# Two split operands of attention: k held twice and rounded whole, with fewer buffers for streamed weights, on one Trainium2 core

## The chip, the cores and the metric

The kernel runs on one core of a Trainium2 chip. The metric is the device time of one execution in microseconds (us); the time shown of a kernel is the median of its runs.

## The reference

Three layers follow one another, all in float32. `moe2_b` and the weights come scaled, which changes no step.

```python
# attention: B, H, S, D = 4, 8, 576, 64; blocks of 64 keys
scores = q @ k.T / sqrt(64)               # per batch and head
scores = where(i // 64 >= j // 64, scores, -1e9)
attn = exp(scores - max); attn = attn / (sum + 1e-9)
x = (attn @ v) -> (2304, 512)
# first layer
h = x @ w_in            # 512 -> 2048
x = maximum(0.01 * h, h) @ w_out          # 2048 -> 512
# second layer
h = x @ w_in
P = a0 + a1*h + a2*h**2 + a3*h**3
Q = 1 + |b0|*|h| + |b1|*h**2
x = (P / (Q + 1e-6)) @ w_out              # (2304, 512)
```

## The kernel before, in words

**Split operands.** The tensor engine multiplies in a rounded form of float32 (F32R). To keep accuracy an operand is split into a high part (rounded) and a low part (what is left, rounded), and a product is made of three matmuls: high by high, high by low, low by high. Weights arrive as int32 pairs; `convert` (L662) loads a block of 512 KB into `cs`, scales its two words, joins them into `cl` on DVE (`cl<-cs`), rounds `cl` to the high part and subtracts for the low part. For the first layer the high parts stay on chip (`w1i`, `w1o`) and the low parts go out to DRAM (`W1L`). For half of the second layer's weights both parts go to DRAM (`W2H`, `W2L`): the high part through a tile `ch`, of which there are two.

**Attention.** There are 32 heads. Heads 0 to 7 (`n < NSF`) are multiplied in plain float32 from tiles `fq` and `fk`. Heads 8 to 31 are split: `load_qk` (L717) loads q into partitions 0 to 63 and k into partitions 64 to 127 of one of two tiles `qk`, and `a1` (L752) makes four tiles from them. QT has the scaled q, rounded, in its lower half of the partitions and its low part in the upper. KH has the rounded k in both halves, made by two operations of 64x576. QM and KL have the rounded q and the low part of k in their lower halves. These tiles take over the storage of `fq` and `fk`, so the trace calls them `split_fq` and `split_fk`. Then `a2_part` makes the scores in tiles `T`, their negated maxima `nm` and the exponentials `PB`; `a2_norm` divides `PB` by its sums `sm`; `a3a` and `a3b` transpose `PB` on PE and evacuate the result (into `acc` for the plain heads, into `pTh` and `pTl` for the split ones); `a4` multiplies with v, which is held in `vr`, or `VHL` when split; `xh` and `xl` are the two parts of the attention's output.

**First layer.** `moe1` (L924) is called for 160 units of twelve matmuls each into a tile `M`: a unit is 128 columns of `w_in` or of `w_out`, for one batch of 512 rows. The last 64 rows of each batch, 256 together, are done at the end, in units of 256 columns (the left-over stage). Every unit streams its low weights, 256 KB, from `W1L` into a tile `wl`; there are six of them. The results `gh` and `gl` of the first half feed the second, whose sums are kept in `acc`, and `x2hd` and `x2ld` in DRAM take the layer's output in two parts.

**Second layer.** `moe2` (L1007) is an ordinary loop. Its first rows come back as `x2h` and `x2l` (1 MB each) while the first layer still runs.

**What sets the order.** Attention, the conversions and the first layer aren't issued as they are written. A recorder keeps every operation with a key (`rec.key`) and, where more than one engine can do it, its forms (`rec.either`). Before they are scheduled, `amend(AMEND)` (L346) steps through a table of entries `step:key:lax:form`: so many operations further on, a number is added to the key or to the leeway, or one form, and so an engine, is fixed. `schedule` then puts the operations in order with a model of costs, and `issue` (L493) writes them out; every recorded instruction therefore bears line L503 in the trace, and its tiles tell it apart. All DMAs of this part go through SP's queue in the order that the schedule gave.

Of the kernel before, what the change touches and what calls it, by code (L numbers as in the profile page):

```python
# [12 lines left out]
F32 = mybir.dt.float32  # L13
F32R = mybir.dt.float32r
# [20 lines left out]
}  # L35

AMEND = """
# [21 lines left out]
"""  # L59


# [465 lines left out]
def attention_moe_moe_kernel(  # L527
# [14 lines left out]
    nc = rec  # L542
    P = 128
    B, H, D, S = q.shape
# [3 lines left out]
    KD = DM // P  # L548
# [19 lines left out]
    def pool(stack, group="all", **kw):  # L568
        return rec.pool(stack, group, **kw)
# [12 lines left out]
    ap = pool(att, "att", name="ap", bufs=1, side="right")  # L582
    xp = pool(ctx, name="xp", bufs=2)
    w1 = pool(ph1, name="w1", bufs=1)
    mp = pool(ph1, name="mp", bufs=2)
    cp = pool(ph1, name="cp", bufs=2)
# [5 lines left out]
    coef = const.tile([P, 6], F32, name="coef")  # L592
    cq = const.tile([P, 1], F32, name="cq")[:, 0:1]

    qk = [ap.tile([P, S], F32, name=f"qk{e}") for e in range(2)]
    vr = [ap.tile([P, 5, P], F32, name=f"vr{j}") for j in range(2)]
    xs = vr[1].rearrange("p t d -> p (t d)")[:, 0:S]

# [5 lines left out]
    QT, QM, KH, KL = {}, {}, {}, {}  # L604
# [31 lines left out]
    NSF = 8  # L636
    E1 = "pvpap"
# [20 lines left out]
    def load_block(i):  # L658
        stage[i] = cp.tile([P, 512, 2], I32, tag="cs", name="cs", bufs=3)
        nc.sync.dma_start(out=stage[i].rearrange("p (r n) w -> p r (n w)", r=KD), in_=blocks[i][0])  # L660

    def convert(i, load, key):  # L662
        rec.key = load
        load_block(i)
        rec.key, rec.lax = key, LAX[0]
        s = stage.pop(i)
        hi, lo = s[:, :, 1], s[:, :, 0]
        nc.scalar.activation(
            hi.bitcast(F32), hi.bitcast(F32), AF.Prelu, scale=2.0 ** -112, alpha=-(2.0 ** 32)
        )  # L670
        rec.either(
            ("ACT", "activation", (lo, lo.bitcast(U32), AF.Copy), {"scale": 0.875 * 2.0 ** -29, "bias": 0.4375}),
            ("POOL", "tensor_scalar", (lo, lo.bitcast(U32), 0.875 * 2.0 ** -29, 0.4375, ALU.mult, ALU.add), {}),
        )
        rec.lax = LAX[1]
        _, (dh, dl), kept = blocks[i]
        f = cp.tile([P, KD, P], F32, tag="cl", name="cl", bufs=3)
        fl = f
        if isinstance(dh, int):
            wh, fl = (  # L680
                x[:, 512 * dl:512 * (dl + 1)].rearrange("p (r c) -> p r c", c=P) for x in W2[dh]
            )
            kept = 2
        else:
            wh = dh if kept else cp.tile([P, KD, P], F32R, tag="ch", name="ch", bufs=2)
        hi, lo = (x.rearrange("p (r c) -> p r c", c=P) for x in (hi, lo))
        nc.vector.scalar_tensor_tensor(
            f.bitcast(I32), hi, 3, lo, ALU.logical_shift_left, ALU.bitwise_or
        )
        rounded(wh, f, "av")  # L690
        subtract(fl if kept == 2 else f.bitcast(F32R), f, wh.bitcast(F32))
        for d, t in () if kept == 2 else ((dh, wh.bitcast(F32)), (dl, f))[kept:]:
            nc.sync.dma_start(out=d, in_=t, also=((), (rec.token("w", i),)))
        rec.lax = 0.0
# [22 lines left out]
    def load_qk(n, second=None):  # L717
        if n >= NHD:
            return
        b, h = divmod(n, H)  # L720
        if n < NSF:
            dq, dk = (T[0:D, :] for T in plain[n % 4])
        else:
            dq, dk = qk[n % 2][0:D, :], qk[n % 2][D:P, :]
        rec.key = LOADKEY(n)
        for c in (slice(0, 192), slice(192, S)) if n == 0 else (slice(0, S),):
            nc.sync.dma_start(out=dq[:, c], in_=q[b, h][:, c])
            (second or nc.sync).dma_start(out=dk[:, c], in_=k[b, h][:, c])

    def load_v(p):  # L730
        b, j = divmod(p, NP)
# [6 lines left out]
    def subtract(out, a, b):  # L738
        rec.either(*((e, "tensor_tensor", (out, a, b, ALU.subtract), {}) for e in ("DVE", "POOL")))

    def rounded(out, in_, engines, by=1.0):
        forms = {
            "a": ("ACT", "activation", (out, in_, AF.Copy), {"scale": by}),
            "v": ("DVE", "tensor_scalar", (out, in_, by, None, ALU.mult), {}),
            "p": ("POOL", "tensor_scalar", (out, in_, by, 1.0, ALU.mult, ALU.mult), {}),
        }
        rec.either(*(forms[e] for e in engines))

    def cp1(eng, out, in_, by=1.0):
        return rounded(out, in_, CH, by)  # L750

    def a1(n):  # L752
        if n < NSF:
            if n > 0:
                fq = plain[n % 4][0][0:D, :]
                cp1("a", fq, fq, SCALE)
            return
        if n < NSF + 2:
            split_tiles(n)
        e = n % 2  # L760
        qs, ks = qk[e][0:D, :], qk[e][D:P, :]
        cp1(E1[0], QT[e][0:D, :], qs, SCALE)
        nc.vector.scalar_tensor_tensor(
            QT[e][D:P, :], qs, SCALE, QT[e][0:D, :].bitcast(F32), ALU.mult, ALU.subtract
        )
        cp1(E1[2], QM[e][0:D, :], QT[e][0:D, :].bitcast(F32))
        cp1(E1[3], KH[e][D:P, :], ks)
        cp1(E1[4], KH[e][0:D, :], ks)
        subtract(KL[e][0:D, :], ks, KH[e][D:P, :].bitcast(F32))

    def a1v(n):
        e = n % 2
# [151 lines left out]
    def moe1(u, load, key):  # L924
        g, kind, i, d = units[u]
        xh, xl = X[g]
        n = NT1 if g < B else B * NL
        if kind == "in":
            wh, s = w1i[:, :, i * P:(i + 1) * P], i
        else:  # L930
            wh, s = w1o[:, 4 * i:4 * i + 4, d * P:(d + 1) * P], NF + 4 * i + d
        rec.key = load
        wl = mp.tile([P, 4, P], F32R, tag="wl", name="wl", bufs=6)
        nc.sync.dma_start(out=wl.bitcast(F32), in_=W1L[s], also=((rec.token("w", BLOCK[s]),), ()))
        rec.key, rec.line = key, 1
        T = psS.tile([P, 512], F32, tag="S", name="M")[:, 0:n]
# [194 lines left out]
    def LOADKEY(n):  # L1131
        return n - 2.8 if n > 2 else n - 20.0
# [3 lines left out]
    for n in range(3):  # L1136
        load_qk(n, nc.scalar)
# [104 lines left out]
    for i in range(len(blocks)):  # L1242
        convert(i, block_key(i) - 1.5, block_key(i))
# [22 lines left out]
    nc = tc.nc  # L1266
# [48 lines left out]
```

## Time and profile before

| | before |
|---|---|
| median of 3 runs | 991.14 us (990.75 to 991.68) |
| the profiled execution | 990.94 us |
| its span | 989.2 us |
| mean granted clock of TensorE | 1.00 |
| PE busy | 977.1 us (99%) |
| DVE, ACT, POOL busy | 735.3, 672.2, 317.6 us |
| DMA traffic | 140.95 MB, 142 GB/s over the span |

The span goes from the first to the last instruction of the profiled execution; what is beyond it in the execution's time is start and end. A trace lists for every instruction when it ran, on which engine, from which tiles, and what ended the idle time before it. PE is the matmul engine, PEld its weight load, DVE, ACT and POOL the three others that compute, SP the one that issues DMAs (SPq is its queue). L503 is the line of the recorder. A group's row gives the instructions' count, their summed busy time and the mean of one in ns.

### The profile page before, as it was taken

The numbers are of one execution on the slowest core, as the hardware profiler recorded it, in microseconds if no ns is written. First come the engines' busy times: TensorE is split into PE (matmuls) and PEld (weight loads), VectorE is DVE, ScalarE is ACT, GpSimd is POOL, SyncE is SP. The second block draws the span as 40 slices with busy tenths as digits, with TensorE's granted clock in tenths as the row PEclk, the third lists the DMA queues.
The fourth block names the chain that finished last, engine by engine and source line by source line (L and its number), as shares of the span: only waits on it lengthen the run. The fifth ranks groups of instructions, "written<-read, shape, count | busy, mean of one in ns | idle before, by whom it ended". The sixth has DMA issues, their size and how long they took to land.

```text
span 989.2 us, 14611 instructions
## 1 busy us (share of the span) xinstructions
PE 977.1 (99%) x4980; PEld 827.1 (84%) x4980; DVE 735.3 (74%) x1244; ACT 672.2 (68%) x1381; POOL 317.6 (32%) x352
## 2 busy tenths in 40 slices
PE   9989999999999999999999999999999999999998
PEld 6768888888888888888888998888888888888896
DVE  5889988887776677555523118999888888888886
ACT  7998989877877667445422328776766766676775
POOL 6778688676654555115203330000000000000000
PEclk9999999999999999999999999999999999999999
DMA  9967878797774542249734759120102101010010
GB/s 207 286 201 240 273 237 272 246 336 229 246 237 143 164 115 69 66 116 328 229 97 125 234 144 386 58 86 0 43 1 86 43 1 43 1 43 1 1 43 23
DMA packets 94923, 140.95 MB, mean 142 GB/s; under 512 B 10368, under 2 KB 47488, under 8 KB 94848
## 3 DMA queue, kind: packets, MB, share of 16 engines
q1 hardware_dynamic: 94368, 139.32, 45.1%
q8 instruction: 39, 0.64, 0.3%
q10 hardware_dynamic: 480, 0.70, 0.2%
q14 instruction: 36, 0.29, 0.1%
HBM read 108.53 MB, written 31.46 MB: 142 GB/s over the span
## 4 chain that ended last, share of the span: by engine, by line
PE 93%; ACT 3%; DMA 2%; DVE 1%; issue 1%; POOL 0%; SPq 0%; ACTq 0%; POOLq 0%; DVEq 0%
PE M L503 40%; PE h L1028 20%; PE o L1082 20%; PE T L503 13%; ACT PB L503 2%; DMA fq<-in_q_dram 1%; DMA vr<-in_v_dram 0%; ACT cs L503 0%; ACT acc L503 0%; POOL PB L503 0%; SPq L503 0%; DMA qk<-in_q_dram 0%; DVE nm L503 0%; DVE xl L503 0%; DVE pTl L503 0%
## 5 line engine op out<-in xcount | busy, mean ns | idle before, releaser
L503 PE MATMUL M<-gh,w1o 128*128 128x512 f32 (+1 forms) x320 | 120.0, 376 | 0.1
L503 PE MATMUL M<-gh,wl 128*128 128x512 f32 (+1 forms) x320 | 118.1, 369 | 0.0
L503 PE MATMUL M<-gl,w1o 128*128 128x512 f32 (+1 forms) x320 | 118.0, 370 | 0.0
L1040 ACT ACTIVATE ea<-h,coef 128x512 f32<-128x512 f32 (+1 forms) x80 | 51.6, 645 | 88.0 <-PE h L1028 88.0
L503 ACT ACTIVATE gf<-M 128x512 f32<-128x512 f32 (+1 forms) x80 | 44.2, 555 | 85.6 <-PE M L503 77.6
L503 ACT ACTIVATE PB<-T,nm 128x448 f32<-128x448 f32 (+4 forms) x160 | 82.6, 524 | 27.6 <-DVE nm L503 27.1
L503 DVE TENSOR_TENSOR acc<-M,acc 128x512 f32<-128x512 f32 (+1 forms) x60 | 38.1, 635 | 71.1 <-PE M L503 70.8
L1028 PE MATMUL h<-x2l,w2h 128*128 128x512 f32 (+1 forms) x240 | 88.3, 368 | 0.0
L1028 PE MATMUL h<-x2h,w2l 128*128 128x512 f32 (+1 forms) x240 | 88.3, 368 | 0.0
L1028 PE MATMUL h<-x2h,w2h 128*128 128x512 f32 (+1 forms) x240 | 88.2, 368 | 0.0
L503 DVE TENSOR_REDUCE nm<-T 128x1 f32<-128x192 f32 (+4 forms) x160 | 71.4, 482 | 19.9 <-PE T L503 19.2
L503 POOL TENSOR_TENSOR gl<-gf,gh 128x512 fp32r<-128x512 f32 (+1 forms) x44 | 50.0, 1137 | 107.5 <-ACT gh L503 97.1
L1082 PE MATMUL o<-w2h,g2h 128*128 128x512 f32 x216 | 84.2, 390 | 0.0
L1082 PE MATMUL o<-w2l,g2h 128*128 128x512 f32 x216 | 84.2, 390 | 0.0
L1082 PE MATMUL o<-w2h,g2l 128*128 128x512 f32 x216 | 84.0, 389 | 0.0
L1043 DVE SCALAR_TENSOR_TENSOR ea<-eh,coef,ea 128x512 f32<-128x512 f32 (+1 forms) x80 | 55.6, 695 | 31.3 <-ACT eh L1041 30.3
L503 PE MATMUL M<-xh,w1i 128*128 128x512 f32 x256 | 75.4, 399 | 0.0
L503 PE MATMUL M<-xl,w1i 128*128 128x512 f32 x256 | 73.3, 391 | 0.0
L503 PE MATMUL M<-xh,wl 128*128 128x512 f32 x256 | 73.1, 391 | 0.0
L503 PEld LDWEIGHTS M<-gl,w1o 128*128 128x128 f32 x320 | 60.3, 189 | 10.5
L503 PEld LDWEIGHTS M<-gh,w1o 128*128 128x128 f32 x320 | 60.4, 189 | 9.0 <-ACT gh L503 0.4
L503 PEld LDWEIGHTS M<-gh,wl 128*128 128x128 f32 x320 | 60.4, 189 | 8.7
(147 smaller groups left out, 2581.1 us busy)
## 6 DMA issues: line engine op xcount, KB each, us to landing
wl<-w1l SPq DMA_DIRECT2D x160, 256.0 KB, 2.9
cs<-in_moe_w_in_dram SPq DMA_DIRECT2D x32, 512.0 KB, 5.4
cs<-in_moe_w_out_dram SPq DMA_DIRECT2D x32, 512.0 KB, 5.2
w1l<-cl SPq DMA_DIRECT2D x32, 256.0 KB, 4.2
vr<-in_v_dram SPq DMA_DIRECT2D x16, 256.0 KB, 3.9
w2h<-ch SPq DMA_DIRECT2D x16, 256.0 KB, 5.3
w2l<-cl SPq DMA_DIRECT2D x16, 256.0 KB, 3.7
x2hd<-xo SPq DMA_DIRECT2D x16, 256.0 KB, 2.9
```

Source lines behind the costliest of these rows:

```text
L503: getattr(self.eng[o.engine], o.name)(*a, **k)
L1028: nc.tensor.matmul(h[:, 0:n], lhsT=a, rhs=x, start=(kk == 0 and i == 0), stop=(kk == KD - 1 and i == 2))
L1040: nc.scalar.activation(a, h, AF.Abs, scale=coef[:, 4:5])
L1043: nc.vector.scalar_tensor_tensor(a, h2, coef[:, 5:6], a, ALU.mult, ALU.add)
L1082: nc.tensor.matmul(ob[t], lhsT=a, rhs=w, start=(f == 0 and i == 0), stop=(f == NF - 1 and i == 2))
```

## The change

In place of one tile with q below and k above, there are a tile `qx` for q and a tile `kk` that k is loaded into twice, once in each half of the partitions. The high part of k is rounded by one operation of 128x576, and the low part is taken from the lower halves. `ch` has one buffer in place of two, `wl` four in place of six. The table AMEND is written anew; its rows are cut here.

```diff
--- before.py
+++ after.py
@@ -35,27 +35,79 @@
 }
 
 AMEND = """
-0:40 3:-17 6:-37 1:11 16:878 3:-154 21:-538 2:-349 7:-126 3::86 3::194 4::62 1::48 4::41 6::78:0 1::79:0 1:::1
...
-1:-252 1:-252 1:-252 1:-252 1:-252 1:-252 1:-252 1:-252 1:-252 1:-252 1:-252 18::81 1::38 15::77 343::10 2::46
+0:40 1:98 1:8 1:14 13:276 1:276 1:276 1:276 18:-23 2:-23 1:-32 3:-59 1:-23 1:-25:567 1:326 1:1 1:43:16 1:-112 1:-592:3
...
+1:-242 1:-242 1:-242 1:-242 1:-242 1:-242 1:-242 1:-75 1:-142
 """
 
 
@@ -592,7 +644,8 @@
     coef = const.tile([P, 6], F32, name="coef")
     cq = const.tile([P, 1], F32, name="cq")[:, 0:1]
 
-    qk = [ap.tile([P, S], F32, name=f"qk{e}") for e in range(2)]
+    qx = [ap.tile([P, S], F32, name=f"qx{e}") for e in range(2)]
+    kk = [ap.tile([P, S], F32, name=f"kk{e}") for e in range(2)]
     vr = [ap.tile([P, 5, P], F32, name=f"vr{j}") for j in range(2)]
     xs = vr[1].rearrange("p t d -> p (t d)")[:, 0:S]
 
@@ -682,7 +735,7 @@
             )
             kept = 2
         else:
-            wh = dh if kept else cp.tile([P, KD, P], F32R, tag="ch", name="ch", bufs=2)
+            wh = dh if kept else cp.tile([P, KD, P], F32R, tag="ch", name="ch", bufs=1)
         hi, lo = (x.rearrange("p (r c) -> p r c", c=P) for x in (hi, lo))
         nc.vector.scalar_tensor_tensor(
             f.bitcast(I32), hi, 3, lo, ALU.logical_shift_left, ALU.bitwise_or
@@ -721,11 +774,13 @@
         if n < NSF:
             dq, dk = (T[0:D, :] for T in plain[n % 4])
         else:
-            dq, dk = qk[n % 2][0:D, :], qk[n % 2][D:P, :]
+            dq, dk = qx[n % 2][0:D, :], kk[n % 2][0:D, :]
         rec.key = LOADKEY(n)
         for c in (slice(0, 192), slice(192, S)) if n == 0 else (slice(0, S),):
             nc.sync.dma_start(out=dq[:, c], in_=q[b, h][:, c])
             (second or nc.sync).dma_start(out=dk[:, c], in_=k[b, h][:, c])
+        if n >= NSF:
+            nc.sync.dma_start(out=kk[n % 2][D:P, :], in_=k[b, h])
 
     def load_v(p):
         b, j = divmod(p, NP)
@@ -758,15 +813,14 @@
         if n < NSF + 2:
             split_tiles(n)
         e = n % 2
-        qs, ks = qk[e][0:D, :], qk[e][D:P, :]
+        qs = qx[e][0:D, :]
         cp1(E1[0], QT[e][0:D, :], qs, SCALE)
         nc.vector.scalar_tensor_tensor(
             QT[e][D:P, :], qs, SCALE, QT[e][0:D, :].bitcast(F32), ALU.mult, ALU.subtract
         )
         cp1(E1[2], QM[e][0:D, :], QT[e][0:D, :].bitcast(F32))
-        cp1(E1[3], KH[e][D:P, :], ks)
-        cp1(E1[4], KH[e][0:D, :], ks)
-        subtract(KL[e][0:D, :], ks, KH[e][D:P, :].bitcast(F32))
+        cp1(E1[3], KH[e], kk[e])
+        subtract(KL[e][0:D, :], kk[e][0:D, :], KH[e][0:D, :].bitcast(F32))
 
     def a1v(n):
         e = n % 2
@@ -930,7 +984,7 @@
         else:
             wh, s = w1o[:, 4 * i:4 * i + 4, d * P:(d + 1) * P], NF + 4 * i + d
         rec.key = load
-        wl = mp.tile([P, 4, P], F32R, tag="wl", name="wl", bufs=6)
+        wl = mp.tile([P, 4, P], F32R, tag="wl", name="wl", bufs=4)
         nc.sync.dma_start(out=wl.bitcast(F32), in_=W1L[s], also=((rec.token("w", BLOCK[s]),), ()))
         rec.key, rec.line = key, 1
         T = psS.tile([P, 512], F32, tag="S", name="M")[:, 0:n]
```

The order of the instructions moves nearly everywhere. Matmuls stay the same in number (4886), and so do POOL's instructions (357); ACT has 1201 in place of 1229, DVE 1250 in place of 1246, SP 524 in place of 500. The engines of the split heads' k rounding are 13 on ACT, 10 on POOL and 1 on DVE in place of 26, 21 and 2. Three places follow, with rows of the order as the program has them. A row is line, operation, output, inputs and the output's shape; the numbers in names tell tiles apart.

The first is ACT's order around the evacuation of a plain head's first transposes, 128x896 into acc, at about 54 us. Before:

```order
L503 ACTIVATE split_fk2_656<-qk1_96 64x576
L503 ACTIVATE PB04_113,sm_664<-T_644,nm_658 128x576
L503 ACTIVATE PB03_112,sm_664<-T_598,nm_658 128x448
L503 ACTIVATE PB02_111,sm_664<-T_632,nm_658 128x320
L503 ACTIVATE PB00_109,sm_664<-T_639,nm_658 128x64
L503 ACTIVATE PB01_110,sm_664<-T_639,nm_658 128x192
L503 ACTIVATE acc_123<-T_673 128x448
L503 ACTIVATE cs_584<-cs_584 128x512
L503 ACTIVATE w1o_122<-cl_681 128x4x128
L503 ACTIVATE PB04_113<-PB04_113,sm_664 128x576
L503 CAST xh_339<-T_650 64x512
L503 ACTIVATE acc_123<-T_677 128x896
```

Now:

```order
L555 ACTIVATE PB14_120<-PB14_120,sm_564 128x576
L555 ACTIVATE PB04_115,sm_666<-T_648,nm_659 128x576
L555 ACTIVATE PB03_114,sm_666<-T_607,nm_659 128x448
L555 ACTIVATE PB00_111,sm_666<-T_634,nm_659 128x64
L555 ACTIVATE PB02_113,sm_666<-T_626,nm_659 128x320
L555 ACTIVATE PB01_112,sm_666<-T_634,nm_659 128x192
L555 ACTIVATE acc_125<-T_672 128x448
L555 CAST xh_341<-T_654 64x512
L555 ACTIVATE acc_125<-T_683 128x896
```

Ahead of the evacuation (the last row of both) a split_fk rounding, a cs conversion, a w1o rounding and the normalisation of PB04 aren't there any more; the normalisation at the beginning, of PB14, is that of another head and stood two rows above the first one shown.

The second is SP's queue where the first rows of the second layer come back (x2h, x2l), behind 436 us; wl are the low weights of consecutive units, cs weights to convert, and xleft the left-over rows. Before:

```order
L503 DMA cab_92<-in_moe2_a_dram 128x4
L503 DMA xleft1_5019<-xld_63 128x1024
L503 DMA cab_92<-in_moe2_b_dram 128x2
L503 DMA wl_5040<-w1l_64 128x512
L503 DMA x2h_5045<-x2hd_61 128x4x512
L503 DMA x2l_5052<-x2ld_62 128x4x512
L503 DMA wl_5060<-w1l_64 128x512
L503 DMA wl_5087<-w1l_64 128x512
L503 DMA cs_5095<-in_moe2_w_in_dram 128x4x256
L503 DMA cs_5101<-in_moe2_w_out_dram 128x1024
L503 DMA wl_5117<-w1l_64 128x512
```

Now:

```order
L555 DMA xleft1_5034<-xld_63 128x1024
L555 DMA cab_92<-in_moe2_a_dram 128x4
L555 DMA cab_92<-in_moe2_b_dram 128x2
L555 DMA wl_5058<-w1l_64 128x512
L555 DMA x2h_5064<-x2hd_61 128x4x512
L555 DMA x2l_5069<-x2ld_62 128x4x512
L555 DMA wl_5079<-w1l_64 128x512
L555 DMA wl_5103<-w1l_64 128x512
L555 DMA cs_5114<-in_moe2_w_in_dram 128x4x256
L555 DMA cs_5120<-in_moe2_w_out_dram 128x1024
L555 DMA wl_5133<-w1l_64 128x512
```

The wl ahead of x2h was that of unit 94 (wl_5040); now it is that of unit 93 (wl_5058), and the one of unit 94 (wl_5079) stands behind x2l.

The third is ACT's order at the last two roundings into ch, at about 279 us. Before:

```order
L503 ACTIVATE PB04_113,sm_3319<-T_3300,nm_3312 128x576
L503 ACTIVATE PB03_112,sm_3319<-T_3332,nm_3312 128x448
L503 ACTIVATE PB02_111,sm_3319<-T_3336,nm_3312 128x320
L503 ACTIVATE pTh_119<-T_3340 128x896
L503 ACTIVATE ch_3370<-cl_3353 128x512
L503 ACTIVATE ch_3377<-cl_3358 128x512
L503 ACTIVATE gf_3385<-M_3351 128x512
L503 ACTIVATE gh_3397<-gf_3385 128x512
```

Now:

```order
L555 ACTIVATE ch_3622<-cl_3526 128x512
L555 ACTIVATE PB12_118<-PB12_118,sm_3427 128x320
L555 ACTIVATE cs_3522<-cs_3522 128x512
L555 ACTIVATE cs_3536<-cs_3536 128x512 x2
L555 ACTIVATE PB04_115,sm_3660<-T_3633,nm_3644 128x576
L555 ACTIVATE PB03_114,sm_3660<-T_3642,nm_3644 128x448
L555 ACTIVATE PB02_113,sm_3660<-T_3648,nm_3644 128x320
L555 ACTIVATE ch_3689<-cl_3668 128x512
```

The two roundings into ch stood next to each other; now seven instructions lie between them (one row holds two).

## Rows read from the trace of the kernel before

**Rows 1.** The page's first line.

```profile
span 989.2 us, 14611 instructions
```

**Rows 2.** Windows: busy us of PE, PEld, DVE, ACT, POOL; clock, DMA share, GB/s.

```profile
50.00:75.00 25.00, 21.43 (x122) 16.40 (x120) 21.61 (x43) 24.32 (x62) 19.14 (x22) 1.00 0.66 203
...
225.00:250.00 25.00, 25.00 (x138) 21.59 (x137) 18.41 (x34) 18.02 (x41) 14.92 (x17) 1.00 0.81 245
...
550.00:575.00 25.00, 25.00 (x211) 25.00 (x210) 3.40 (x8) 8.02 (x20) 6.71 (x11) 1.00 0.69 209
```

**Rows 3.** Timeline of PE: start, us, what, [idle before <- releaser]; 50 to 80 us.

```profile
54.72 1.24 PE L503 MATMUL T<-fk,fq 128*128 128x288 f32 x4 [1.54 <-ACT acc L503]
...
63.00 0.66 PE L503 MATMUL T<-ident,PB 128*128 128x128 f32 x4 [0.97 <-ACT PB L503]
...
68.53 2.09 PE L503 MATMUL T<-ident,PB 128*128 128x128 f32 x14 [0.43 <-DVE acc L503]
...
71.06 3.08 PE L503 MATMUL T<-acc,vr 128*128 128x128 f32 x12 [0.44 <-ACT acc L503]
...
78.79 1.06 PE L503 MATMUL T<-ident,PB 128*128 128x128 f32 x8 [1.16 <-DVE acc L503]
```

**Rows 4.** Groups by form of ACT, 0 to 110 us: busy, mean ns | idle.

```profile
L503 ACT ACTIVATE cs<-cs 128x512 f32<-128x512 f32 x21 | 14.3, 686 | 0.1
...
L503 ACT ACTIVATE acc<-T 128x896 f32<-128x896 f32 x7 | 6.5, 927 | 0.4 <-PE T L503 0.3
...
L503 ACT ACTIVATE PB<-PB,sm 128x576 f32<-128x576 f32 x7 | 5.5, 789 | 0.0
L503 ACT ACTIVATE w1i<-cl 128x512 fp32r<-128x512 f32 x8 | 5.1, 642 | 0.0
...
L503 ACT ACTIVATE acc<-T 128x320 f32<-128x320 f32 x6 | 2.6, 434 | 0.0
...
L503 ACT ACTIVATE fq<-fq 64x576 f32<-64x576 f32 x3 | 2.0, 678 | 1.3 <-DMA fq<-in_q_dram 1.3
L503 ACT ACTIVATE PB<-PB,sm 128x448 f32<-128x448 f32 x3 | 2.0, 674 | 0.3 <-DVE sm L503 0.3
...
L503 ACT ACTIVATE PB<-PB,sm 128x64 f32<-128x64 f32 x5 | 1.8, 358 | 0.0
...
L503 ACT ACTIVATE split_fk<-qk 64x576 fp32r<-64x576 f32 x2 | 1.4, 680 | 0.1
```

**Rows 5.** Groups by form of DVE, 0 to 110 us.

```profile
L503 DVE SCALAR_TENSOR_TENSOR cl<-cs 128x512 int32<-128x512 int32 x20 | 18.1, 915 | 0.5 <-DMA w1l<-cl 0.2
```

**Rows 6.** Groups by form over the span: the roundings of k.

```profile
L503 POOL TENSOR_SCALAR split_fk<-qk 64x576 fp32r<-64x576 f32 x21 | 18.0, 857 | 5.8 <-DVE pTl L503 4.1 <-POOL cl L503 0.2
L503 ACT ACTIVATE split_fk<-qk 64x576 fp32r<-64x576 f32 x25 | 17.1, 683 | 5.2 <-PE T L503 4.6
```

**Rows 7.** PE's waits: us in total, times, longest.

```profile
PE T L503 <- POOL PB L503: 1.3, 2, 0.9
```

**Rows 8.** Timeline of PE in unit 94.

```profile
452.48 0.39 PE L503 MATMUL M<-gh,w1o 128*128 128x512 f32 x1
452.71 0.39 PE L503 MATMUL M<-gh,wl 128*128 128x512 f32 x1
```

**Rows 9.** The loads of wl issued from 549 to 583 us: duration ns, landing us.

```profile
L503 SPq DMA_DIRECT2D wl<-w1l x24: 319/319/319, 549.5 to 582.5; - x24
...
DMA to landing us min/median/max: 2.5/2.7/3.8
```

**Rows 10.** Timeline of SP behind 439 us.

```profile
439.27 0.37 SPq L503 DMA_DIRECT2D x2h<-x2hd  x1
...
441.79 3.05 SPq L503 DMA_DIRECT2D wl<-w1l  x2
```

**Rows 11.** DMA issues from 441.7 to 442.1 us: KB, us to landing.

```profile
wl<-w1l SPq DMA_DIRECT2D x1, 256.0 KB, 8.9
```

**Rows 12.** DMA issues from 200 to 300 us: KB, median us to landing.

```profile
w2h<-ch SPq DMA_DIRECT2D x13, 256.0 KB, 5.2
```

90 rows, old and new, of the table AMEND are left out of this document.

## The prediction

> **What bounds the kernel now.** I read the page's first line and the busy shares by stretch first, then the timeline of PE, then the list of what PE waited for, and last the busy groups of ACT, DVE and POOL. The profiled execution took 990.94 us, of which 989.2 are the span [rows 1]; the median of the runs is 991.14, so 0.2 us are added to every sum below to reach a median. From about 125 us on PE is busy all the time: 25.00 of 25 us in the attention stretch and in the left-over stage [rows 2], and the change leaves its matmuls as they are. So nothing after that is to be gained, unless PE begins it earlier. In the stretch from 50 to 75 us it is another engine that ends last: ACT is busy 24.32 of 25 us and PE 21.43 [rows 2]. The timeline of PE shows where that comes through: five waits, 1.54, 0.97, 0.43, 0.44 and 1.16 us, 4.54 together, three of them for ACT's evacuations (acc) or normalisations (PB), two for DVE's evacuations [rows 3]. Each us that ACT and DVE have less to do ahead of these five places starts all the later matmuls earlier.
>
> **The change part by part.**
>
> *One rounding of k instead of two.* Of each split head (24 of them) two 64x576 roundings go, 0.683 us where ACT does one and 0.857 where POOL does [rows 6], and one of 128x576 comes. No row has that; the nearest is ACT's normalisation of the same shape, 0.789 [rows 4]. Its bounds are 0.683, if only the columns count, and 1.54, the two old ones together. I take 0.79, so a head saves 0.75 us and 24 heads 18 us of engine time. Nearly all of it lies behind 125 us, where PE waits for no one [rows 2], and is worth nothing there. What counts is the part ahead of the five waits, and what the new order does with the rest.
>
> *Work ahead of the five waits.* I counted ACT's and DVE's instructions up to the one that releases PE, in the order before and in the new one, and priced the differences.
> - Release of the wait at 54.72 (the 128x896 evacuation): 83 instructions ahead before, 79 now. Two cs conversions fewer (-1.37), one fq (-0.68), one split_fk and one split_fq (-0.68 each), one PB 128x576 (-0.79), one w1i rounding (-0.64); one PB 128x64 (+0.36), one acc 128x320 (+0.43), one acc 128x896 (+0.93) more [rows 4]. Sum -3.1 us.
> - Release at 63.00 (PB 128x192): two cs (-1.37), one fq and four split roundings of 64x576 (five of 0.68, -3.4) fewer; one PB 128x576, one 128x448, one 128x64 (+0.79, +0.67, +0.36) and one acc 128x896 (+0.93) more; a w1i less and a w1o more cancel [rows 4]. Sum -2.0 us.
> - Release at 71.06 (128x896): counted in the same way, with three w1i roundings fewer in place of one, -3.7 us.
> - Release at 78.79 (DVE): eight instructions fewer ahead; two conversions cl<-cs make 1.8 us of it [rows 5], and 0.37 us each for the other six would be enough for what follows.
>
> Each wait is a bound: release plus all the PE work behind it. Today the last one binds, and the bound of an earlier one lies below it by the waits that follow. So the bounds fall by 3.1+3.00 = 6.1 (54.72), 2.0+2.03 = 4.0 (63.00), 3.7+1.16 = 4.9 (71.06) and over 4.0 (78.79); by what stands ahead of 54.72 at most all five waits can go, 4.54. The least counts: **-4.0 us**. The wait at 68.53 I could not price, since PE's own order differs there; its bounds are 0 and 0.43 of this.
>
> *k loaded twice.* 24 more DMAs of 144 KB on SP's queue. At the rate of 50 to 75 us (203 GB/s at a share of 0.66, so 308 at full share) [rows 2] each takes 0.48 us of the DMA engines, 11.5 us in all. PE waits for no DMA anywhere in its list, whose largest entries are engines, with POOL's PB at 1.3 [rows 7]. I cost it at 0; the cover is the second tile, loaded while the other head is at work. If it were gone, one late load would cost PE its 0.48.
>
> *wl from 6 buffers to 4.* A low weight block is now asked for three units ahead instead of five. Of 512-column units three are 36 matmuls, 0.23 apart [rows 8], 8.2 us of cover; in the left-over stage, with 211 matmuls in 25 us [rows 2], a unit is 1.42 us and three are 4.27, against landings of at most 3.8 plus 0.32 to issue [rows 9]. So 0, with 0.15 us to spare: this is the thinnest cover of the change.
>
> *x2 burst behind 439 us.* Today x2h goes out at 439.27, after the load for unit 94; the next wl behind the 2 MB follows at 441.79 [rows 10] and lands 8.9 us later, at 450.7 [rows 11]. In the new order the pair goes out one unit later and the load of unit 94 stands behind it. One unit is 12 x 0.23 = 2.7 us, so it lands at about 453.4 against its first use at 452.71 [rows 8]. Bounds are 0 (the DMA engines are freer by then) and 4.0 (all of the following loads one after another late); I take the shift, rounded down because the queue starts emptier: **+0.5**.
>
> *One ch buffer.* A rounding into ch now waits until the w2h transfer has read the last one, 5.2 us from issue to landing [rows 12]. The order spreads these roundings: the closest pairs have 6, 7 and 8 instructions between them, at about 0.65 us [rows 4] 3.9, 4.6 and 5.2 us. That leaves 1.3+0.6+0 = 2 us of ACT's time, perhaps 4 with the issue. ACT is busy 18.02 of 25 us there [rows 2], so most of it falls into idle time. Between 0 and 4 I take **+0.5**.
> The Trainium skill says under "Trainium Kernel Development and Optimization", section Best Practices, to double-buffer so that DMA overlaps with compute, which speaks against this edit; by that rule the full 4 us would show, rival C. The trace of before has two buffers and cannot show it.
>
> Sum: -4.0+0.5+0.5 = -3.0, from 990.94 to 987.9, as a median 988.1. With the ends of the terms, -4.54 and -2.0, this case alone runs from 986.6 to 989.1.
>
> **The rivals.**
> - **B, the new order keeps it all.** All five waits go, the two later terms are nothing, and the 1.3 us for POOL's PB [rows 7] go too, since POOL also has less k to round: 990.94-4.54-1.3+0.2 = 985.3. For it: POOL's 0.857 is the dearer form [rows 6]. Against: those two waits come ahead of the first split head.
> - **C, the gain is given back behind the attention.** One ch buffer costs its 4 us, or the x2 burst its 4: 990.94-4.0+4.0+0.2 = 991.1; with half of that 989. For it: ACT's and DVE's streams run in order, so a stalled rounding holds the evacuation behind it. Against: PE has not waited there once.
> - **E, the waits only change their place.** The change doesn't do what it seems to: if PE's waits come from the round trip scores, exponential, transposes, evacuation and not from ACT's load, fewer instructions ahead release nothing earlier, and 991 stays. For it: two of the five waits are for DVE, which is less full than ACT. Against: 24.32 of 25 [rows 2].
> - **D, the left-over stage starves (slower).** Four buffers give one unit in (1.42+0.32+L)/4 us, with L from issue to landing. At 3.8 that is 1.39, under 1.42; it decides from L of 3.94 on. At L = 5, which the extra pressure of late loads could bring, a unit takes 1.69, 0.27 more, and over 26 units 7 us: 995. For it: the margin of 0.15 us [rows 9]. Against: the median landing there is 2.7. To come out slower than before it must eat 3 us, so L over 4.4 throughout.
>
> **How the numbers follow.** The forecast has 0.45, B 0.16, C and E 0.13 each, D 0.13. A measurement tells about 0.2%, 2 us, from no change: faster is below 989.2, slower above 993.1. Forecast and B are faster (0.61); of C and E together 0.01 more; the rest of them, 0.25, and 0.01 of D are the same (0.26); D's other 0.12 is slower. So 0.62, 0.26 and 0.12. The range goes from 984.5, a little under B, to 992.0, a little over C and E; it leaves out D and a few hundredths beyond B. The likeliest case's own range is the 986.6 to 989.1 above.
>
> **What would show it.** Right: in the stretch from 50 to 75 us PE's busy time rises above 21.43 toward 24, the waits in [rows 3] shrink to about half a us in all, and the first matmul of a given unit in the second half comes 3 to 4 us earlier; the 128x576 rounding takes about 0.8 us. PE stays at 25.00 of 25 in the left-over stage, and at most about 0.5 us of PE idle stands near unit 94, with ACT or DVE waiting a little for w2h's transfer. Wrong: PE waits on wl in the left-over stage (D); an idle of several us near 450 or waits for ch on ACT that PE's list answers to (C); five waits of the same sum between 50 and 80 us (E); or a rounding of 1.2 us or more, which would take most of the 18 us back.

## The result, and the profile after

The changed kernel takes 996.34 us (median of 6 runs, 995.32 to 998.76), the kernel before 991.24 in the same comparison: a ratio of 1.0055, with a 95% interval of 1.0045 to 1.0065. It is slower by 5 us, where 3 us less were forecast. The profiled execution took 996.11 us, its span is 994.3.

The second layer has no part in it. These are PE's first matmuls of that layer, in the timeline of the kernel before and in that of the changed one:

```profile
591.12 0.40 PE L1028 MATMUL h<-x2h,w2h 128*128 128x512 f32 x1
```

```profile
596.27 0.40 PE L1082 MATMUL h<-x2h,w2h 128*128 128x512 f32 x1
```

They lie 5.15 us apart, and from there to the end both take 398.0. So all of it is lost before. The waits of PE in the changed kernel (what it waited for: us in total, times, longest):

```profile
PE T L555 <- POOL PB L555: 2.8, 2, 2.0
PE T L555 <- ACT PB L555: 2.6, 4, 1.0
PE T L555 <- ACT acc L555: 1.7, 2, 1.3
PE warm L555 <- DVE cq L555: 1.2, 1, 1.2
PE M L555 <- DMA wl<-w1l: 1.1, 1, 1.1
```

And its busy time by stretch, in the columns of [rows 2]; behind it one more stretch of the kernel before:

```profile
50.00:75.00 25.00, 23.03 (x129) 17.72 (x127) 18.12 (x40) 22.62 (x58) 17.09 (x21) 1.00 0.62 186
100.00:125.00 25.00, 23.78 (x127) 19.29 (x126) 22.73 (x39) 19.36 (x44) 15.25 (x15) 1.00 0.77 240
175.00:200.00 25.00, 22.97 (x115) 19.77 (x114) 18.75 (x29) 18.39 (x40) 18.48 (x17) 0.93 0.78 249
225.00:250.00 25.00, 25.00 (x135) 21.60 (x135) 19.63 (x37) 18.70 (x44) 16.57 (x18) 1.00 0.84 268
550.00:575.00 25.00, 25.00 (x204) 24.73 (x203) 3.44 (x8) 7.82 (x19) 8.43 (x10) 1.00 0.77 233
```

```profile
175.00:200.00 25.00, 25.00 (x137) 21.42 (x136) 22.01 (x35) 21.26 (x49) 17.52 (x17) 1.00 0.78 240
```

Against [rows 2] the stretch from 50 to 75 us has gained as meant: PE 23.03 for 21.43, ACT 22.62 for 24.32. What is new is 175 to 200 us, with 2.03 us of PE idle and a granted clock of 0.93, where PE had been busy throughout. The timeline of PE has the places:

```profile
29.68 1.24 PE L555 MATMUL T<-fk,fq 128*128 128x288 f32 x4 [1.30 <-ACT acc L555]
...
62.09 0.66 PE L555 MATMUL T<-ident,PB 128*128 128x128 f32 x4 [0.77 <-ACT PB L555]
63.38 3.08 PE L555 MATMUL T<-acc,vr 128*128 128x128 f32 x12 [0.64 <-ACT PB L555]
...
69.69 3.08 PE L555 MATMUL T<-acc,vr 128*128 128x128 f32 x12 [0.35 <-ACT acc L555]
...
109.81 0.33 PE L555 MATMUL T<-ident,PB 128*128 128x128 f32 x1 [0.96 <-ACT PB L555]
...
184.98 1.93 PE L555 MATMUL T<-ident,PB 128*128 128x128 f32 x8 [2.03 <-POOL PB L555]
...
457.69 0.50 PE L555 MATMUL M<-gh,wl 128*128 128x512 f32 x1 [1.07 <-DMA wl<-w1l]
```

To add up what each place costs, every matmul of a trace is charged with the median spacing of its shape and kind (plain, transposing or split) in the kernel before (0.227 us for one of 512 columns), and PE's lag at a matmul is its start less what the matmuls ahead were charged. The lag in us, by the work that PE has behind it:

| us of PE work done | 20 | 45 | 70 | 100 | 165 | 170 | 430 | 435 |
|---|---|---|---|---|---|---|---|---|
| before | 5.3 | 6.2 | 13.2 | 14.4 | 15.5 | 15.6 | 20.5 | 20.5 |
| changed | 4.3 | 6.9 | 10.7 | 14.3 | 15.7 | 19.6 | 24.3 | 25.6 |
| run dve_order | 4.3 | 7.2 | 11.0 | 12.4 | 14.0 | 14.1 | 21.1 | 22.3 |
| run x2_late | 5.1 | 6.2 | 9.9 | 13.5 | 15.0 | 19.0 | 24.1 | 24.0 |
| run all_three | 4.7 | 6.0 | 9.8 | 11.3 | 12.8 | 12.9 | 18.0 | 18.0 |

Between 45 and 70 the changed kernel loses 3.8 where the one before lost 7.0: the gain is there, 3.2 us. By 100 it is given back (the waits at 28 and 109 us among others). Then 3.9 go at one place, at 183 us, and 1.3 at 457, behind the x2 burst. All the rest runs alike.

What happens at 183 us stands in the timelines of DVE and POOL in the changed kernel:

```profile
173.77 2.40 DVE L555 SCALAR_TENSOR_TENSOR cl<-cs 128x512 int32<-128x512 int32 x1
176.09 0.68 DVE L555 TENSOR_TENSOR acc<-M,acc 128x512 f32<-128x512 f32 x1
176.80 3.39 DVE L555 SCALAR_TENSOR_TENSOR split_fq<-qx,split_fq 64x576 fp32r<-64x576 f32 x1
180.22 0.75 DVE L555 TENSOR_TENSOR vr<-T,vr 64x576 f32<-64x576 f32 x1
...
182.63 0.17 DVE L555 RECIPROCAL sm<-sm 128x5 f32<-128x5 f32 x1
...
183.22 1.27 DVE L555 SCALAR_TENSOR_TENSOR cl<-cs 128x512 int32<-128x512 int32 x2
```

```profile
174.31 1.30 POOL L555 TENSOR_TENSOR cl<-cl,w1o 128x512 fp32r<-128x512 f32 x1
175.57 1.89 POOL L555 TENSOR_TENSOR split_fk<-kk,split_fk 64x576 fp32r<-64x576 f32 x1
177.43 1.29 POOL L555 TENSOR_TENSOR cl<-cl,w1o 128x512 fp32r<-128x512 f32 x1
178.69 0.88 POOL L555 TENSOR_TENSOR VHL<-vr,VHL 128x320 fp32r<-128x320 f32 x1
182.90 2.02 POOL L555 TENSOR_SCALAR PB<-PB,sm 128x448 f32<-128x448 f32 x1 [3.33 <-DVE sm L555]
```

DVE's subtraction for split_fq reads two operands of SBUF. It takes 0.74 us at its quickest in this trace, and 3.39 here. POOL runs three subtractions without a pause, to 179.57, and DVE's ends 0.62 us after that, at 180.19. Everything behind it on DVE is 2.6 us late, sm among it; for sm waits POOL's PB (3.33), and for that PE (2.03). A second hold, of POOL by DVE, adds to it: this normalisation of PB takes 2.02 us, where twelve of its fourteen in this trace take 0.64, and DVE's two conversions at 183.22 lie within it. With 0.64 PE's wait would have been about 0.65 us (an estimate, 2.03 less the 1.38).

The clock makes it dearer. By windows of 2 us (in the columns of [rows 2]):

```profile
182.00:184.00 2.00, 0.95 (x5) 0.45 (x3) 2.00 (x7) 1.73 (x5) 1.10 (x1) 1.00 0.79 251
184.00:186.00 2.00, 1.02 (x5) 1.03 (x6) 0.52 (x2) 2.00 (x7) 1.44 (x2) 0.77 0.75 200
186.00:188.00 2.00, 2.00 (x11) 1.82 (x10) 0.41 (x1) 1.52 (x3) 1.28 (x1) 0.50 0.97 335
188.00:190.00 2.00, 2.00 (x13) 1.82 (x12) 1.74 (x3) 1.83 (x4) 1.12 (x2) 0.88 0.96 338
```

After the idle time PE goes on at the lower of its two levels (1.2 GHz, 0.50) until about 188 us. So 2.03 us of waiting cost 3.9 us of lag. Not every execution pays that: in the profiles of x2l_later and fq_later the same wait (2.00 and 1.99 us) passes at 1.00 and costs 2.3 and 2.4 us. The other runs of the changed kernel agree: those with a mean clock of 0.999 and 1.000 took 995.32 and 995.40, those with 0.997 took 998.25 and 998.76.

### The profile page after: what moved, and what is told of

Read it like the earlier page. It is cut to its first block, busy times and chain, and to the rows that moved or that the text cites. A ratio compares the mean times of both kernels' runs of the same rounds, so it can differ in the third digit from the quotient of the medians.

```text
span 994.3 us, 14617 instructions
## 1 busy us (share of the span) xinstructions
PE 979.2 (98%) x4980; PEld 827.0 (83%) x4980; DVE 740.7 (74%) x1248; ACT 655.0 (66%) x1353; POOL 315.1 (32%) x352
## 4 chain that ended last, share of the span: by engine, by line
PE 88%; DVE 3%; DMA 3%; ACT 3%; issue 1%; SPq 1%; POOL 0%; ACTq 0%; DVEq 0%; POOLq 0%
PE M L555 37%; PE h L1082 20%; PE o L1136 20%; PE T L555 12%; ACT PB L555 2%; DMA fq<-in_q_dram 1%; DMA wl<-w1l 1%; DVE split_fq L555 1%; DVE cl L555 1%; SPq L555 1%; DMA fk<-in_k_dram 0%; DVE nm L555 0%; ACT cs L555 0%; ACT acc L555 0%; DMA qx<-in_q_dram 0%
## 5 line engine op out<-in xcount | busy, mean ns | idle before, releaser
L555 ACT ACTIVATE PB<-T,nm 128x320 f32<-128x320 f32 (+4 forms) x160 | 82.7, 524 | 31.2 <-DVE nm L555 30.7
L555 DVE TENSOR_REDUCE nm<-T 128x1 f32<-128x320 f32 (+4 forms) x160 | 71.2, 482 | 24.3 <-PE T L555 23.6
L555 POOL TENSOR_TENSOR gl<-gf,gh 128x512 fp32r<-128x512 f32 (+1 forms) x46 | 54.7, 1192 | 75.3 <-ACT gh L555 54.4
L555 PE MATMUL T<-ident,PB 128*128 128x128 f32 x480 | 65.0, 278 | 5.0 <-POOL PB L555 2.8
```

The lines of the kernel that those rows point to most:

```text
L555: getattr(self.eng[o.engine], o.name)(*a, **k)
```

## The experiments

Two theories. **Theory 1:** the new order costs, by DVE held behind POOL, with the x2 burst as a loss of its own. **Theory 2:** the parts cost (one ch, four wl, k loaded twice). To move an operation without planning anew, a helper takes recorded operations (by number) out of the finished order and puts them behind another; to undo a part without planning anew, the finished order is kept and only the real tiles or instructions are altered. The first two lines below are of pool_string, the other two of old_parts:

```diff
-    order = rec.schedule(slack=200.0, late=600.0, bank=300.0)
+    order = moved(rec.schedule(slack=200.0, late=600.0, bank=300.0), [((2545, 2546, 1090), 1066)])
...
-            kw.update(tag=s.tag, bufs=s.bufs)
+            kw.update(tag=s.tag, bufs={'ch': 2, 'wl': 6}.get(s.tag, s.bufs))
```

The kernel before took 991.04 to 991.24 in these comparisons.

| run | median us | ratio to before (95%) |
|---|---|---|
| pool_string | 995.95 | 1.0045 (1.0032 to 1.0058) |
| old_parts | 995.57 | 1.0042 (1.0030 to 1.0054) |
| old_k | 995.08 | 1.0034 (1.0022 to 1.0046) |
| x2l_later | 994.39 | 1.0030 (1.0019 to 1.0041) |
| x2_late | 994.34 | 1.0036 (1.0024 to 1.0047) |
| dve_order | 992.01 | 1.0010 (1.0001 to 1.0019) |
| all_three | 989.14 | 0.9981 (0.9973 to 0.9990) |
| buffers_alone | 996.57 | 1.0055 (1.0041 to 1.0069) |
| fixed_old_k | 992.60 | 1.0015 (1.0006 to 1.0024) |
| fixed_old_parts | 992.98 | 1.0019 (1.0010 to 1.0028) |
| fq_later | 997.14 | 1.0059 (1.0046 to 1.0072) |
| act_too | 988.44 | 0.9974 (0.9964 to 0.9983) |

**pool_string**, the first line of the diff above.

> The changed kernel with two POOL subtractions and one DMA (the low parts of a w1o block and of VHL, 177.4 to 179.6 us in its trace, and the block's write to W1L) issued behind the two normalisations of PB that PE waits for at 183 us; nothing else moves. Theory 1, DVE held by POOL's unbroken string: split_fq's subtraction on DVE (3.39 us there) ends when POOL pauses, so it shrinks to 1.2 to 1.8 us, PE's wait of 2.03 falls under 0.3, the clock stays at 1.00 there, and the time falls by 3 to 4.5 us, to about 992.3. Theory 2, the parts of the change (one ch, four wl, k loaded twice) make DVE late there: nothing changes, 996.3 within 0.7.

The mechanism came out, the time did not. DVE's row, from the timeline of this run:

```profile
177.06 1.28 DVE L555 SCALAR_TENSOR_TENSOR split_fq<-qx,split_fq 64x576 fp32r<-64x576 f32 x1
```

POOL now pauses at 177.72, and DVE's operation ends at 178.34, again 0.62 us later. PE's wait at 183 us is gone, and the lag at 170 us of work is 15.95 for 19.61. But the lag then grows by 1.9 up to 200 us of work, where the changed kernel loses 0.5: 0.9 between 186 and 190 us with no wait in PE's list, and 0.7 at 198 us, where PE waits for POOL's gl (0.40 us, and 0.39 in dve_order and all_three, whose POOL order is untouched). And at the x2 burst PE, there earlier, waited longer:

```profile
457.33 0.80 PE L555 MATMUL M<-gh,wl 128*128 128x512 f32 x1 [2.83 <-DMA wl<-w1l]
```

With the clock at 0.50 behind it that place cost 4.5 us in place of 1.3. So there are two losses, and in this execution the second takes what the first gives back. It was the longest of its six (993.11 to 997.17), so the others may have lost less there.

**old_k**: k goes back to the upper half of q's tile; in the issue of the finished order its second load is left out and its rounding given as two instructions. **old_parts**: the same, and the second part of the diff.

> The changed kernel's order of instructions kept one for one, but with the parts of the kernel before: q and k in one tile, k loaded once, its high part rounded by two 64x576 operations on the engine that the order gives, two ch and six wl tiles. Theory 1 (the new order is what costs, by DVE held behind POOL): the wait near 183 us stays or grows, since POOL's string gets a second rounding, and the time stays at 995 to 999. Theory 2 (the parts cost it): it falls to 991 to 992.

> As the run with the old parts, but ch and wl keep their new numbers of tiles, so only the loading and rounding of k is undone under the new order. Theory 1: 996 to 999, a little above the changed kernel, since each head has one rounding more on ACT or POOL (0.68 to 0.86 us) and the order has no room for it. Theory 2, in the form that the second load of k makes DMAs and so DVE late: 991 to 993.

Both stay near the changed kernel, at 995.57 and 995.08 for 996.34, far from 991, so the parts aren't the main cost and Theory 2 falls. Theory 1 was not borne out as it stood either: the wait at 183 us was to stay or grow, and it is not there with the old k; old_k, expected a little above the changed kernel, came a little below. PE loses at 170 and 197 us instead (waits of 0.39, 0.42 and 1.06 us in old_k, for DVE's pTl and acc and for POOL's gl). With six wl tiles the load of unit 94 was out right behind x2l, and PE still lost 1.7 us waiting for it: it is the place behind 2 MB, not the number of tiles. That run waited for a wl in the left-over stage too (0.94 us at 559 us), which no run with four tiles does.

**x2l_later** and **x2_late**: `[((5273,), 4242)]`, and `[((5272,), 4568), ((5273,), 4600)]`.

> The changed kernel with the 1 MB load x2l issued behind the wl of unit 94 instead of ahead of it. That wl landed 9.4 us after its issue and PE waited 1.07 us for it at 457 us. If the burst is the cause, it lands about 2.7 us earlier, the wait is gone, no later wl comes late, and the time falls by 1.0 to 1.3 us, to 995.1; if wl is late because only four tiles exist (the issue at 448.26 is late), the wait stays.

> The changed kernel with the two 1 MB loads x2h and x2l issued some 18 and 20 units later, at about 500 and 505 us, where the DMA engines are a third busy and well ahead of the 582 us at which the second layer begins; nothing else moves. If the burst is a loss of its own, the wait for wl at 457 us (1.07 us in the changed kernel's profile, 2.99 with a fall of the clock where PE comes there earlier) is gone altogether, and the time falls by 1.4 to 4 us, to 993 to 995, below the run with x2l alone moved. If the four wl tiles are the cause, the wait stays at about 1 us.

Both medians are 2.0 us lower, with intervals (up to 1.0041 and 1.0047) at the edge of the changed kernel's (from 1.0045). In the profile of the first, the wait at unit 94 falls to 0.17 us, but 0.45 us of lag are still lost there and 0.7 at a later unit, 1.2 in all for 1.4 in the changed kernel; its lower median is therefore not shown to come from the burst. In the second, which was to come out below the first and did not, no wait for wl is left, and the lag does not move between 430 and 435 us of work. By that profile the burst is a loss of its own, of 1.4 us; the four tiles are not.

**dve_order**: `[((684, 759), 700), ((1071, 1142), 1061)]` (759 and 1142 are the next loads into the tile that is read).

> The changed kernel with the two subtractions of split_fq that DVE held longest for (4.00 us at 98.6, 3.39 us at 176.8) issued a few instructions later on DVE, behind operations that read PSUM (nm, vr) and the two short ones on sm; POOL's order is not touched. Theory 1 (DVE's SBUF operation waits for a pause of POOL, and what stands behind it waits with it): PE's waits at 108.5 (0.96) and 183 us (2.03) shrink by over 1 us together in the first and nearly all in the second, the lag of PE at 190 us is 3 to 5 us smaller, and the time is 991.5 to 994, the rest being the x2 burst. Theory 2 (POOL's PB normalisations themselves are late, since POOL has too much to do): the waits stay.

Measured 4.3 us less, 992.01. The subtraction, now behind the short operations on sm, meets a pause of POOL:

```profile
179.16 0.18 DVE L555 RECIPROCAL sm<-sm 128x5 f32<-128x5 f32 x1
179.37 0.75 DVE L555 SCALAR_TENSOR_TENSOR split_fq<-qx,split_fq 64x576 fp32r<-64x576 f32 x1
```

POOL's own work and order are those of the changed kernel, and both waits, at 109 and 183 us, are gone. So POOL was not short of time; DVE's order was what made it late. Of the 5.5 us that this profile has gained at 170 us of work 2.3 are lost again by 430, with waits of 0.39, 0.44 and 0.69 us at 196, 219 and 310 us; all_three keeps only the first of them.

**all_three**: the moves of x2_late and dve_order, and `((293,), 214)`. **fq_later**: the last alone.

> Both of these together, and the scaling of fq that ACT held 1.95 us for at 26 to 28 us (its load came then) issued behind the 128x896 evacuation that PE waits for (1.30 us there). If the three are separate losses, their sum comes off the changed kernel: 3 to 5 us for DVE, 1.4 to 4 for the burst, about 1 for fq, so 989 to 991, at or below the kernel before. If one only hides another, it stays above 992.

> The changed kernel with the scaling of fq on ACT alone moved behind the evacuation. PE's wait at 28 us (1.30 us in the profile of the changed kernel) goes, 0.7 to 1.5 us come off, unless the DVE stalls behind it swallow them: 994.8 to 995.6 if not, 996.3 if so.

All three together give 989.14, the sum of the parts (4.3 and 2.0 from 996.34 leave 990.0) and a little more, and faster than the kernel before. The share of fq is not settled: alone it gave nothing in the median (997.14, slower than either outcome expected), though the wait at 28 us was absent in its profile, which is that of its fastest run (994.83). In the profile of x2_late that wait is absent too, with fq where it was, since the load of fq came earlier in that run.

**buffers_alone**: `bufs=6` to `bufs=4` and `bufs=2` to `bufs=1` in the kernel before.

> The kernel before with four wl and one ch tile, its table and k as they were; the order is planned anew for these numbers. Theory 2 (fewer buffers cost): 994 to 998, with PE waiting for wl. Theory 1: what the plan moves decides; waits for wl outside the x2 burst do not occur, and one ch costs ACT 1 to 4 us of waiting and PE at most 1, so 990.5 to 993.

This missed: 996.57, as slow as the changed kernel, and in the range that Theory 2 gave. But the order is planned anew in it, and its profile, that of its fastest run (a span of 992.4), loses 1.4 us behind the x2 burst as well, with wl, and waits for wl nowhere else. PE's waits for ACT's PB come to 4.0 us in it, for 1.0 in the kernel before; what else it loses was not taken apart. The tiles without a new plan are priced by the next pair.

**fixed_old_k** and **fixed_old_parts**: old_k and old_parts with the moves of all_three.

> The kernel with all three places moved, and k loaded once and rounded by two 64x576 operations as before, under the same order; ch and wl keep one and four tiles. It prices the change of k itself where the order has no big stall. If the one rounding is worth engine time that PE sees, the time rises by 0.5 to 3 us over the run with all three (989.1), to 990 to 992; if the second load of k costs as much as it gives, it stays within 0.5 us.

> The same with two ch and six wl tiles as well, so all parts of the kernel before under the new order with the three places moved. If the fewer tiles cost something there, it is faster than the run with the old k alone by over 0.5 us; if they don't (no wait for wl left, ACT's wait for ch off PE's path), the two agree within 0.5 us.

The two agree within 0.4 us, so two ch and six wl tiles are worth nothing here. And both are 3.5 to 3.8 us slower than all_three (the kernel before took 991.04 and 991.05 in the two comparisons), more than the 0.5 to 3 expected. So k's part as a whole (a tile of its own, the second load, one rounding) is worth that much under this order. But the order was planned for it, and with the old k PE waits again where it did in old_k:

```profile
171.24 0.58 PE L570 MATMUL T<-pTl,VHL 128*128 128x128 f32 x2 [0.41 <-DVE pTl L570]
...
172.44 0.51 PE L570 MATMUL M<-gh,w1o 128*128 128x512 f32 x1 [0.41 <-DVE acc L570]
...
198.72 0.50 PE L570 MATMUL M<-gl,w1o 128*128 128x512 f32 x1 [1.06 <-POOL gl L570]
```

That is fixed_old_k; all_three has one wait there, of 0.39 us. Between 100 and 200 us of work fixed_old_k loses 5.2 us and all_three 2.7. Under the order as it was, the median of old_k came out 1.3 us below the changed kernel's; here the old k is 3.5 us slower. What the part is worth hangs on the order. The new k under the order of the kernel before was not run.

**act_too**: all_three and `((2397,), 450), ((2408,), 512), ((2401,), 505)`.

> All three places moved, and on ACT between 58 and 68 us one rounding of w1o and two conversions of cs issued behind the normalisation and the exponentials of PB that PE waits for (waits of 0.78, 0.63 and 0.36 us there). If those waits are ACT's order and no more, 0.6 to 1.5 us come off the run with all three: 987.7 to 988.6; if another engine ends last right behind ACT, nothing.

988.44, a little less than all_three (988.44 to 990.86 there, 987.86 to 989.21 here), near the weak end of what was expected. The two intervals overlap, and both profiled executions span 986.6, so a gain is not shown. The wait at 61 us fell from 0.78 to 0.27, the next two stayed:

```profile
61.01 0.66 PE L555 MATMUL T<-ident,PB 128*128 128x128 f32 x4 [0.27 <-ACT PB L555]
62.25 3.08 PE L555 MATMUL T<-acc,vr 128*128 128x128 f32 x12 [0.58 <-ACT PB L555]
...
68.54 3.08 PE L555 MATMUL T<-acc,vr 128*128 128x128 f32 x12 [0.35 <-ACT acc L555]
```

It has the lowest median of all, 0.26% below the kernel before.

## Why the prediction was wrong

- **One rounding in place of two**: right. The 128x576 rounding takes 0.682 us on ACT and 0.760 on POOL, for 0.79 forecast, and the two engines spend 16.5 us on it in place of 35.1 [rows 6], 18.6 less for 18 forecast. DVE took 10.3 us back: its 24 subtractions for split_fq went from 24.5 to 34.8 us. The groups by form of the changed kernel:

```profile
L555 ACT ACTIVATE split_fk<-kk 128x576 fp32r<-128x576 f32 x13 | 8.9, 682 | 3.7 <-PE T L555 3.7
L555 POOL TENSOR_SCALAR split_fk<-kk 128x576 fp32r<-128x576 f32 x10 | 7.6, 760 | 5.4 <-PE T L555 5.2
```

- **The five waits, -4.0**: right at its place, too large. The waits between 50 and 80 us fell from 4.54 [rows 3] to 1.76, the lag by 3.2. But the sum took the rest of the first 115 us as unchanged, and it was not: 1.5 us of lag went at 28 us, where ACT stood before a load of fq with the evacuation behind it, and about as much at 109 us. At 100 us of PE work nothing was left of it. That these places would stay quiet was not worked out.
- **"Nearly all of it lies behind 125 us, where PE waits for no one, and is worth nothing there"**: the step that failed most. It was read as "nothing to be gained", and the sum then had no term for what could be lost there. The stretches behind 125 us were quiet in the old order, and the order is new everywhere. 3.9 us went at 183 us, where DVE stood behind POOL and POOL then behind DVE; with DVE's order changed there and at 98 us, 4.3 us came back (dve_order).
- **The durations**: DVE's conversion was priced by the mean of its row, 0.915 [rows 5]. Such a row holds waits: the 20 in it run from 0.67 to 2.37 us, and the subtraction for split_fq has a mean of 1.45 us in the changed kernel and 1.02 in the one before, for 0.74 and 0.75 at its quickest. That DVE stands while POOL runs was not among the rivals, though the scheduler of both kernels reckons with it (`shares_port`). Rival C, the gain given back, came nearest in kind, but it put the loss on ch or the x2 burst; the burst is a quarter of it, ch nothing.
- **The x2 burst, +0.5**: right mechanism, undersized. The load of unit 94 landed 9.4 us after its issue at 448.26, as [rows 11] had it for the one before (8.9); the wait of 1.07 and its restart cost 1.3 us of lag, and 4.5 in pool_string, a little over the bound of 4.0. The shift was rounded down "because the queue starts emptier", but the load took 0.5 us longer to land than the one before.
- **One ch, +0.5**: ACT waited 2.3 us for w2h, as worked out (2 to 4), and no wait of PE leads back to it; fixed_old_k against fixed_old_parts prices it with wl at nothing. The rule of the Trainium skill on double buffering ("Trainium Kernel Development and Optimization", Best Practices), by which rival C would have shown, did not decide here. ACT's group, with the idle time ahead of it:

```profile
L555 ACT ACTIVATE ch<-cl 128x512 fp32r<-128x512 f32 x13 | 8.1, 624 | 2.3 <-DMA w2h<-ch 2.3
```

- **wl at four, and rival D**: right that it costs nothing. PE is busy 25.00 of 25 us in the left-over stage.
- **k loaded twice, 0**: not contradicted. PE waits for no load of k; no run undoes the second load by itself.

With three places of the order moved, the change does come out at 989.14, near the 988.1 of the forecast; but the forecast was for the order as it is, and there the gain was lost.

## What to carry to other kernels

When a change comes with a rewritten order, price the places that are quiet now as well: a rewritten order can lose anywhere, and one stall of 2 us cost up to 4 here. Where two engines hold each other up, read the quickest and the longest of an operation beside its mean, and put the operation that can be held behind those that someone waits for. Large loads that no one needs soon go away from a stream with short cover: moving x2h and x2l some 60 us later took PE's wait for wl away, with 2 us off the median. And price a part in the order that it will have: the old k was no slower in one order and 3.5 us slower in the other.

## What the runs showed of the hardware

- DVE's operations on two SBUF operands stand while POOL works, sometimes for several POOL instructions on end. In the changed kernel's trace 12 of the 24 subtractions for split_fq take over 1 us (0.74 at the quickest, 4.00 at most), and each of the 12 ends 0.61 to 0.67 us after the end of a POOL instruction. Four of them, at 98.6, 158.6, 176.8 and 291.5 us, stood through what was left of one POOL instruction and the next two; others, as at 129.1 us (1.73), got in after the first. A pause of POOL is not needed: at 98.6 us the next POOL instruction followed at once, and took 1.44 us where one of its shape takes 0.88. It goes the other way too: POOL's PB of 2.02 us at 182.90 ended 0.42 us after the two DVE conversions that began at 183.22 (to 184.50).
- The Trainium skill says under "SBUF — State Buffer", section "SBUF: two separate sides", that DVE and GpSimd share a pair of ports as an exclusive lock, held for a whole instruction, by which the loser blocks; the traces agree, and show that a waiting DVE may be passed over by more than one instruction.
- PE's idle times of 2.03 and 2.83 us were followed by a granted clock of 0.50 (1.2 GHz) for 3.4 us, so that they cost 3.9 and 4.5. In the profiles of x2l_later and fq_later idle times of 2.00 and 1.99 us at the same place passed at 1.00; in that of x2_late one of 2.02 did not.
- A 64x576 and a 128x576 rounding take the same on ACT: 0.683 [rows 6] and 0.682 us.
